# Weight loads by a list of units, and query rows loaded two pairs ahead

## The chip, the core and the metric

The kernel runs on one core of a Trainium2 chip. The core has five engines that run at the same time and wait for one another through semaphores: PE (TensorE, matrix products; its weight loads are shown as PEld), DVE (VectorE), ACT (ScalarE), POOL (GpSimd) and SP (SyncE, which here only issues transfers). Transfers between the large memory (DRAM) and the on-chip memory (SBUF) run on 16 DMA engines. SP, ACT and POOL each issue transfers in the order of their own instructions: an instruction that waits holds up all that stand behind it on its engine.

The metric is the device time of one execution in microseconds (us); lower is better.

## What is computed

Two independent parts, joined along the last axis. Part A is a long convolution (an SSM layer): a shift filter on k, a product with v, a convolution over the sequence of 2048 with ssm_k, and a product with q. Part B is a recurrent attention over 64 segments of 32 rows, each of which carries 8 memory rows on to the next.

```python
def _A_ref(q, k, v, shift_k, ssm_k, ssm_D):
    ...
    kv = k_shift * v
    ...
    kv_f = rfft(kv_pad); kf_f = rfft(kf_pad)
    y = irfft(kv_f * kf_f)[:, :S, :]
    y = y + kv * ssm_D[None, None, :]
    return q * y

def _B_ref(x, mem0, Wq, Wk, Wv, Wo, seg_len):
    ...
    for s in range(n_seg):
        h = concat([mem, x[:, s * 32:(s + 1) * 32]])
        q, k, v = h @ Wq, h @ Wk, h @ Wv
        p = softmax(mask(q @ k.T * scale))
        o = (p @ v) @ Wo
        mem = o[:, :M]; outs.append(o[:, M:])
```

## The kernel before

Part A is a Fourier transform in factors, in three stages, each a loop over tiles of 128 rows. Stage 1 (`a_kernel`, up to about 105 us) transforms the rows of u = kv and of the filter and stores them to DRAM as SU1 and SK1. Stage 2 (lines 290 to 399) has 17 sets; for each set SP gathers four tiles of 0.26 MB (Kg and Ug, three buffers each), and the set is worked on in two halves. One half is called a unit here, so there are 34, numbered 0 to 33. A unit has a front (PE makes Kre, Kim, Ure and Uim in PSUM, ACT and DVE multiply them, POOL makes Yre, DVE makes Yim) and a back, one unit later (PE makes z_ps from Yre and Yim, ACT copies it to zs; after the second half ACT stores zs to SZ in DRAM). Stage 3 (lines 401 to 422) has 16 tiles: SP loads zt from SZ (0.52 MB; all of SZ must be there, as each zt reads a strip across all sets), PE makes y_ps with four matmuls, DVE multiplies it with the query rows qt, and POOL stores the product of two tiles at a time (ot to out). A qt holds the query rows of two tiles, a pair.

Between these PE does work of part B. `fill` (line 675) is called once per unit in stage 2 and once per tile in stage 3, and counts its calls in n: n = 0 to 33 are the units, n = 34 to 49 the tiles. Each call stores one finished piece of the dense part (RKQ, on ACT), may copy a weight from SBUF to a scratch in DRAM (WS, on POOL), may load a weight (`load_next`, line 659), transposes x rows at every third n (`x_block`, xt_ps on PE, stored to REC by POOL; X_sb is loaded by `x_load` two blocks at a time), and advances the generator `rest` by one to three slices. A slice is four matmuls kb_ps on PE. `rest` runs four dense groups: Wk first half, Wk second half, Wq first half, Wq second half, 32 slices each, and each needs eight weights of 0.52 MB.

The first group's weights are loaded by POOL at the end of stage 1. The other 24 are in `plan` (line 649), in the order in which the groups need them, with a home for each: tiles Wmid, which stay; three spare tiles; ring tiles pw; and last the tile wring2, which holds x rows (X_sb) as long as stage 2 lasts. `stage1_done` issues four of the 24 loads and twelve slices ahead of unit 0. `fill` issues the others by a rule (line 686): at each n below 34 that doesn't leave 2 on division by 3, as long as more than two are left, and the last two at n = 37 and 38. The load is placed behind the newest gather on SP. Loads of weights that are streamed later are followed by their copy to WS at an odd n; a copy waits for its load.

PE's order in stage 2 is written out by hand (`manual_schedule`). All other orders are made by a scheduler from the program and the tiles' lifetimes: PE's in stage 3, and SP's, POOL's, DVE's and ACT's everywhere. A tile that takes over the place of an older one waits until that one's readers and writers are done; stage 3's pools take the places of stage 2's, and the homes of the Wv weights (Wres, Wmore, loaded by SP after the last zt) those of stage 3's.

After stage 3 PE finishes the dense groups and computes vb_ps from the Wv weights (line 775). From about 383 us on the recurrence of part B runs, 64 segments, in which PE streams weights that stay in SBUF and 13 per segment that SP loads anew (wring from WS).

Of the kernel before, what the change touches and what calls it, by code (L numbers as in the profile page):

```python
# [9 lines left out]
BF = mybir.dt.bfloat16  # L10
# [18 lines left out]
STREAM = (0, 8, 15, 19, 24, 31, 36, 41, 45, 51, 52, 54, 56, 57, 58, 63)  # L29
N2, N3 = 12, 19  # L30
WO_COPY = 29
AHEAD, REST_LOAD = 12, (37, 38)
X_LOAD = 1
STAGE3 = 34
LATE_RING = 5
# [17 lines left out]
def a_kernel(ctx: ExitStack, tc, q, k, v, shift_k, ssm_k, ssm_D, outa, ps_sum, slot4, slot16, stage1_done, fill):  # L53
    nc = tc.nc
# [18 lines left out]
    def pair_rows(ap2d, t):  # L73
        return ap2d.rearrange("(p r) d -> p (r d)", r=16)[:, 1024 * t:1024 * t + 2048]

    with ExitStack() as c1:
        cw = c1.enter_context(tc.tile_pool(name="a_cw", bufs=1, side="right"))
        io = c1.enter_context(tc.tile_pool(name="a1_io", bufs=2, side="right"))
# [320 lines left out]
            unit_back(*pending)  # L399

    with ExitStack() as c3:
        io = c3.enter_context(tc.tile_pool(name="a3_io", bufs=4, side="right"))
        wk = c3.enter_context(tc.tile_pool(name="a3_wk", bufs=4, side="right"))
        ps_big = c3.enter_context(tc.tile_pool(name="a3_ps", bufs=3, space=PSUM))
        xp = c3.enter_context(tc.tile_pool(name="a3_x", bufs=2, side="right"))
        for t in range(16):
            pt = ps_big.tile([128, 1024], F32, tag="big", name="y_ps")
            zt = io.tile([128, 2, 1024], BF, tag="zt", bufs=5, name="zt")
            nc.sync.dma_start(zt[:], SZ.rearrange("m (r h) d -> r m h d", h=2)[t])
            for hf in range(2):  # L410
                for h in range(2):
                    nc.tensor.matmul(pt[:, hf * 512:(hf + 1) * 512], lhsT=G2h[h][:, :],
                                     rhs=zt[:, h, hf * 512:(hf + 1) * 512], start=(h == 0), stop=(h == 1))
            if t % 2 == 0:
                qt = io.tile([128, 2048], BF, tag="qt", bufs=3, name="qt")
                nc.sync.dma_start(qt[:], pair_rows(q, t))
                ot = wk.tile([128, 2048], BF, tag="ot", name="ot")
            half = slice(1024 * (t % 2), 1024 * (t % 2) + 1024)
            nc.vector.tensor_tensor(out=ot[:, half], in0=pt[:], in1=qt[:, half], op=ALU.mult)
            if t % 2:  # L420
                nc.gpsimd.dma_start(outa.rearrange("(p r) d -> p r d", r=16)[:, t - 1:t + 1, :],
                                    ot[:].rearrange("p (r d) -> p r d", r=2))
            fill(pool=xp)


def b_kernel(ctx: ExitStack, tc, x, mem0, Wq, Wk, Wv, Wo, outb, n_seg, run_a):
    nc = tc.nc
# [28 lines left out]
    def dram_chunk(ch):  # L456
        m, a, g = ch
        return Wo_v[a] if m == 3 else W_v[m][a, g]

    def dst_view(ap, ch):  # L460
        return ap.rearrange("p (hh d) -> p hh d", hh=2) if ch[0] == 3 else ap

    def stream_src(ch):
        return WS[ring_order.index(ch), :, 0:2048]
# [47 lines left out]
    def stage1_done(su, vl, spare):  # L512
        make_consts()
        pools["mid"] = ctx.enter_context(tc.tile_pool(name="b_wmid", bufs=1, reuse_waits="tile"))
        for i, ch in enumerate(parts[0]):
            res[ch] = pools["mid"].tile([128, 2048], BF, name=f"Wmid{i}")[:]
        make_xbt(su)
        ws = [None] * 8
        for kc in range(8):
            with tc.issue_after(vl[1 + kc // 3].ins):  # L520
                group(0, 0, which=[kc], ws=ws, eng=nc.gpsimd)
        weights[0, 0] = ws
        plan_loads(spare)
        for _ in range(4):
            load_next()
        for _ in range(AHEAD):
            next(rest)

# [31 lines left out]
    def make_xbt(su):  # L560
        xb = x.rearrange("(tb s t) d -> tb s t d", s=16, t=SEG)
        for tb in range(4):
            X_sb = pair()[:, 0:1024]
            with tc.issue_after(su[X_LOAD + tb].ins):
                nc.sync.dma_start(X_sb, xb[tb, :, NX:SEG, :])
            tp = ps0.tile([128, 1024], BF, tag="ps0", name="xbt_ps")
            for kc in range(8):
                nc.tensor.transpose(tp[:, kc * 128:(kc + 1) * 128], X_sb[:, kc * 128:(kc + 1) * 128], ident[:])
            for h in range(2):
                nc.scalar.copy(XBT[h][:, :, 16 * tb:16 * tb + 16, :].rearrange("p k s t -> p k (s t)"),  # L570
                               tp[:, 512 * h:512 * h + 512].rearrange("p (k c) -> p k c", k=4))
# [3 lines left out]
    def group(m, g, temps={}, which=range(8), ws=None, eng=nc.sync, held=False):  # L575
        ws = ws or [None] * 8
        for kc in which:
            ch = (m, kc, g)
            if ch in res:
                got.append(eng.dma_start(res[ch], dram_chunk(ch)))  # L580
                ws[kc] = res[ch]
            else:
                t = temps[ch]() if ch in temps else pw()
                got.append(eng.dma_start(t[:], dram_chunk(ch)))
                if ch in streamed:
                    copies.append((stream_src(ch), t[:]))
                ws[kc] = t[:]
        while copies and not held:
            copied.append(nc.gpsimd.dma_start(*copies.pop(0)))
        return ws  # L590
# [4 lines left out]
    def x_load(b, pool=None):  # L595
        t = pool.tile([128, 2048], BF, tag="X_sb", name="X_sb") if pool else base.tile([128, 2048], BF, tag="wring2", name="X_sb")
        x_loads.append(nc.sync.dma_start(t[:].rearrange("p (b d) -> p b d", b=2),
                                         x[b * 128:(b + 2) * 128, :].rearrange("(b p) d -> p b d", b=2)))
        loaded[b], loaded[b + 1] = t[:, 0:1024], t[:, 1024:2048]
# [42 lines left out]
    plan = []  # L642

    def plan_loads(spare):
        pws = iter((4, 5, 6, 7, 0, 1))
        temps = iter([lambda: spare(0), lambda: spare(1), lambda: spare(2), lambda: pw(3), lambda: pw(2),
                      lambda: base.tile([128, 2048], BF, tag="wring2", name="pw")])
        for m, g in ((0, 1), (1, 0), (1, 1)):
            for kc in sorted(range(8), key=lambda kc: (m, kc, g) not in placed):
                ch = (m, kc, g)  # L650
                plan.append((ch, (lambda k=next(pws): pw(k)) if ch in kept_q1 else None if ch in placed else next(temps)))

    def load_next(ins=None):
        ch, home = plan.pop(0)
        m, kc, g = ch
        if ch in kept_q1:
            res[ch] = home()[:]
        with tc.issue_after(ins) if ins is not None else ExitStack():
            group(m, g, {ch: home}, [kc], weights[m, g], held=True)
# [8 lines left out]
    def store():  # L668
        if stores:
            nc.scalar.dma_start(*stores.pop(0))  # L670
# [5 lines left out]
    def fill(behind=None, pool=None):  # L676
        store()
        n = units[0]
        units[0] += 1
        if n == 0:  # L680
            x_load(0)
        if n >= WO_COPY and wo_copies:
            ch = wo_copies.pop(0)
            with tc.issue_after(rec_stores[-1].ins):
                nc.gpsimd.dma_start(dst_view(stream_src(ch), ch), dram_chunk(ch))
        if n in REST_LOAD or n < STAGE3 and n % 3 != 2 and len(plan) > len(REST_LOAD):
            load_next((behind or x_loads[-1]).ins)
        if n > 5 and n % 2 and copies:
            with tc.issue_after(rec_stores[-1].ins):
                copied.append(nc.gpsimd.dma_start(*copies.pop(0)))  # L690
        if n % 3 == 2 and blocks:
            b = blocks.pop(0)
            x_block(b, pool)
            if b % 2 and blocks:
                x_load(b + 1, pool)
        for _ in range(3 if n >= STAGE3 else 1 if n % 3 == 2 else 2):
            next(rest, None)

    run_a(ps0, pw, slot16, stage1_done, fill)

    wres3 = ctx.enter_context(tc.tile_pool(name="b_wres", bufs=1, reuse_waits="tile"))
# [463 lines left out]
def kernel(  # L1165
# [23 lines left out]
    def run_a(ps_sum, slot4, slot16, stage1_done, fill):  # L1189
        with ExitStack() as ctx_a:  # L1190
            a_kernel(ctx_a, tc, A_q[0], A_k[0], A_v[0], A_shift_k, A_ssm_k, A_ssm_D, outa, ps_sum, slot4, slot16, stage1_done, fill)
# [41 lines left out]
```

## Time and profile before

| | us |
|---|---|
| three runs | 1717.8, 1718.3, 1725.6 |
| their median | 1718.33 |
| the profiled run | 1718.1 |
| its span, first to last instruction | 1716.2 |
| PE busy in the span | 1639.0 (96%) |
| DVE busy | 1031.3 (60%) |
| ACT busy | 681.3 (40%) |
| POOL busy | 349.9 (20%) |
| mean DMA rate | 348 GB/s |

Times in a profile count from the first instruction. A busy time is the sum over an engine's instructions; matmuls overlap, so a busy PE can have short gaps inside. "Idle before" is the time for which an engine stood still just ahead of an instruction, and behind the arrow stands what released it. The chain of waits follows the end of the program back to the beginning, at each step to whatever came last. A table of windows gives for each stretch of time its length, the busy time of each engine with the number of instructions, the granted clock of PE as a share of full speed, the mean share of time in which the 16 DMA engines were busy (somewhat over 1.00 is possible, as packets overlap), and the bytes that they moved. For a DMA the profile gives the time from its issue to its landing.

### The profile page before, as it was taken

The numbers are of one execution on the slowest core, as the hardware profiler recorded it, in microseconds if no ns is written. First come the engines' busy times: TensorE is split into PE (matmuls) and PEld (weight loads), VectorE is DVE, ScalarE is ACT, GpSimd is POOL, SyncE is SP. The second block draws the span as 40 slices with busy tenths as digits, with TensorE's granted clock in tenths as the row PEclk, the third lists the DMA queues.
The fourth block names the chain that finished last, engine by engine and source line by source line (L and its number), as shares of the span: only waits on it lengthen the run. The fifth ranks groups of instructions, "written<-read, shape, count | busy, mean of one in ns | idle before, by whom it ended". The sixth has DMA issues, their size and how long they took to land.

```text
span 1716.2 us, 71129 instructions
## 1 busy us (share of the span) xinstructions
PE 1639.0 (96%) x30744; PEld 998.9 (58%) x30776; DVE 1031.3 (60%) x3454; ACT 681.3 (40%) x1259; POOL 349.9 (20%) x626
## 2 busy tenths in 40 slices
PE   6888898999999999999999999999999999999998
PEld 3433333445666666666666666666666666666665
DVE  9947873235555665665565555565665556555555
ACT  6876661103333333433333333333333333333333
POOL 4103341101212121121121121211211211212111
PEclk9999999999999999999999999999999999999999
DMA  9989989989999999999999999999999999999997
GB/s 332 378 321 366 384 291 411 381 319 381 351 338 355 355 351 344 358 349 350 353 344 346 339 344 351 352 355 337 357 355 340 346 340 361 350 346 352 340 330 282
DMA packets 180830, 598.03 MB, mean 348 GB/s; under 512 B 24658, under 2 KB 24674, under 8 KB 180516
## 3 DMA queue, kind: packets, MB, share of 16 engines
q1 hardware_dynamic: 151860, 525.80, 84.4%
q0 software_dynamic: 19984, 44.61, 7.4%
q10 hardware_dynamic: 8672, 23.07, 3.4%
q8 instruction: 241, 3.95, 0.9%
q14 instruction: 73, 0.60, 0.1%
HBM read 538.33 MB, written 57.15 MB: 347 GB/s over the span
## 4 chain that ended last, share of the span: by engine, by line
PE 80%; DMA 10%; DVE 3%; ACT 3%; issue 3%; POOL 1%; SPq 0%; ACTq 0%; another core or an unknown queue 0%; DVEq 0%; POOLq 0%
PE acc L967 36%; PE yacc L1061 27%; PE kb_ps L630 4%; PE vb_ps L775 2%; DMA zt<-SZ 2%; DMA wring<-WS 2%; PE OTp L989 2%; DMA out_dram<-arena 2%; PE OTp L1039 2%; PE OTp L905 1%; ACT s_sb L249 1%; DMA Ug<-SU 1%; PE s_ps L247 1%; PE SB L995 1%; PE ks_ps L285 1%
## 5 line engine op out<-in xcount | busy, mean ns | idle before, releaser
L967 PEld LDWEIGHTS <-rec 128*32 128x32 bf16 x12288 | 301.7, 96 | 278.2 <-DVE rec L916 37.6
L1061 PEld LDWEIGHTS <-arena 128*64 128x64 bf16 x8255 | 430.2, 109 | 54.1 <-ACT arena L1051 32.7
L980 ACT CAST arena<-acc 128x512 bf16<-128x512 f32 x320 | 187.1, 585 | 357.3 <-PE acc L967 347.7
L967 PE MATMUL acc<-Wres,rec 128*32 128x512 bf16 x3328 | 252.7, 380 | 0.7 <-issue 0.7
L967 PE MATMUL acc<-wring,rec 128*32 128x512 bf16 x2300 | 229.5, 380 | 4.6 <-DMA wring<-WS 1.8
L967 PE MATMUL acc<-Wmid,rec 128*32 128x512 bf16 x3072 | 211.8, 379 | 0.2 <-issue 0.2
L1061 PE MATMUL yacc<-Wmore,arena 128*64 128x256 bf16 (+1 forms) x2560 | 209.5, 273 | 0.2 <-issue 0.2
L1051 ACT CAST arena<-OTp 128x640 bf16<-128x640 f32 x128 | 88.6, 692 | 204.7 <-PE OTp L1043 185.1
L1092 DVE COPY arena<-OTp 128x512 bf16<-128x512 bf16 x64 | 27.2, 425 | 229.3 <-PE OTp L905 229.3
L1061 PE MATMUL yacc<-wring,arena 128*64 128x256 bf16 x2064 | 160.0, 274 | 3.1 <-DMA wring<-WS 2.5
L813 DVE TENSOR_SCALAR arena<-OTp 128x256 int32<-128x256 int32 x378 | 128.1, 394 | 37.1 <-ACT arena L1051 34.7
L1061 PE MATMUL yacc<-arena 128*64 128x256 bf16 x1071 | 140.1, 270 | 0.1
L1158 ACT CAST arena<-yacc 128x256 bf16<-128x256 f32 x128 | 47.7, 373 | 228.7 <-PE yacc L1061 225.4
L967 PE MATMUL acc<-pw,rec 128*32 128x512 bf16 x1796 | 122.3, 379 | 1.6 <-issue 1.5
L946 POOL DMA_DIRECT2D arena<-VBD x128 | 68.6, 536 | 261.2 <-DVE arena L1006 94.8
L967 PE MATMUL acc<-Wlate,rec 128*32 128x512 bf16 x1536 | 117.0, 381 | 0.0
L916 DVE CAST rec<-tps 128x32 bf16<-128x32 f32 x128 | 24.5, 192 | 149.7 <-PE tps L914 148.6
L1160 POOL DMA_DIRECT2D out_dram<-arena x128 | 66.0, 516 | 203.9 <-ACT arena L1158 200.2
L900 POOL DMA_DIRECT2D arena<-RKQ x64 | 49.7, 777 | 257.1 <-PE yacc L1061 248.1
L1004 DVE TENSOR_REDUCE mx<-SB 128x8 f32<-128x320 f32 x128 | 62.6, 489 | 49.3 <-PE SB L998 46.3
L895 POOL DMA_DIRECT2D rec<-REC x64 | 36.0, 563 | 244.4 <-PE acc L967 240.4
L1009 ACT ACTIVATE arena<-arena 128x320 f32<-128x320 f32 x128 | 60.3, 471 | 64.2 <-DVE arena L1006 60.2
(222 smaller groups left out, 2628.5 us busy)
## 6 DMA issues: line engine op xcount, KB each, us to landing
wring<-WS SPq DMA_DIRECT2D x831, 512.0 KB, 5.9
SK<-s_sb SPq DMA_DIRECT2D x16, 512.0 KB, 7.4
SU<-s_sb SPq DMA_DIRECT2D x16, 512.0 KB, 6.4
Kg<-SK SPq DMA_DIRECT2D x32, 256.0 KB, 6.2
Ug<-SU SPq DMA_DIRECT2D x32, 256.0 KB, 6.5
RKQ<-stage ACTq DMA_DIRECT2D x16, 512.0 KB, 8.2
zt<-SZ SPq DMA_DIRECT2D x16, 512.0 KB, 10.2
arena<-RKQ POOLq DMA_DIRECT2D x64, 128.0 KB, 5.7
```

Source lines behind the costliest of these rows:

```text
L630: nc.tensor.matmul(ps[:], lhsT=ws[kc][:, hl * 128:(hl + 1) * 128], rhs=xbt(kc).rearrange("p s t -> p (s t)"), start=(kc == 0), stop=(kc == 7))
L813: nc.vector.tensor_scalar(out=dst, in0=src, scalar1=0, scalar2=None, op0=ALU.bitwise_or)
L900: nc.gpsimd.dma_start(rec.rearrange("p (j c) -> p j c", j=4), RKQ[s // 16, :, :, s % 16, :].rearrange("j p c -> p j c"))
L946: nc.gpsimd.dma_start(VB, VBD[g, s].rearrange("t h e -> h t e"))
L967: nc.tensor.matmul(self.acc[32 * c:32 * c + 32, :], lhsT=hT[:, ch[1], :], rhs=w[:, 512 * c:512 * c + 512], start=(ch == chs[0]), stop=(ch ...
L980: nc.scalar.copy(sb, self.acc[:])
L1004: nc.vector.tensor_reduce(out=mx[:], in_=S, op=ALU.max, axis=AX.X)
L1009: nc.scalar.activation(E, E, ACT.Exp, scale=scale)
L1051: nc.scalar.copy(OT, o_view)
L1061: nc.tensor.matmul(yacc[f][64 * dh:64 * dh + m, x - o:y - o], lhsT=lhsT, rhs=r, start=(h == (0, 2 * FIRST[-1])[f] and x == o), stop=stop, ...
L1158: nc.scalar.copy(Y[:, 256 * f:256 * f + 256], yacc[f][:, 0:256])
L1160: nc.gpsimd.dma_start(bass.AP(outb.tensor, outb.offset + SEG * s * 2048 + 512 * dh, [[2048, 32], [1, 512]]), Y[64 * dh + NM:64 * dh + 40, :])
```

## The change

The rule for the weight loads is replaced by a list, `LOAD_AT`, with one entry per load: the n at which it is issued. The four loads in `stage1_done` are gone; units 28 to 33 each have an entry, unit 33 two, and the last load is at n = 35. In stage 3 the pools are entered in another order: ot's pool first, then a new pool for qt with three buffers that waits by the tile, then zt's with five buffers, and x rows last as before. Two qt are loaded ahead of the loop and, at each even tile t up to 10, the one for the pair t + 4; before, each pair's qt was loaded behind its first zt.

```diff
-AHEAD, REST_LOAD = 12, (37, 38)
+AHEAD = 12
+LOAD_AT = (0, 1, 2, 3, 4, 6, 8, 10, 12, 14, 16, 18, 20, 22, 24, 26, 28, 29, 30, 31, 32, 33, 33, 35)
...
     with ExitStack() as c3:
-        io = c3.enter_context(tc.tile_pool(name="a3_io", bufs=4, side="right"))
         wk = c3.enter_context(tc.tile_pool(name="a3_wk", bufs=4, side="right"))
+        qp = c3.enter_context(tc.tile_pool(name="a3_q", bufs=3, side="right", reuse_waits="tile"))
+        io = c3.enter_context(tc.tile_pool(name="a3_io", bufs=5, side="right"))
         ps_big = c3.enter_context(tc.tile_pool(name="a3_ps", bufs=3, space=PSUM))
         xp = c3.enter_context(tc.tile_pool(name="a3_x", bufs=2, side="right"))
+        def q_load(t):
+            qt = qp.tile([128, 2048], BF, tag="qt", name="qt")
+            nc.sync.dma_start(qt[:], pair_rows(q, t))
+            return qt
+
+        qts = [q_load(0), q_load(2)]
         for t in range(16):
             pt = ps_big.tile([128, 1024], F32, tag="big", name="y_ps")
-            zt = io.tile([128, 2, 1024], BF, tag="zt", bufs=5, name="zt")
+            zt = io.tile([128, 2, 1024], BF, tag="zt", name="zt")
...
             if t % 2 == 0:
-                qt = io.tile([128, 2048], BF, tag="qt", bufs=3, name="qt")
-                nc.sync.dma_start(qt[:], pair_rows(q, t))
+                qt = qts.pop(0)
+                if t < 12:
+                    qts.append(q_load(t + 4))
                 ot = wk.tile([128, 2048], BF, tag="ot", name="ot")
...
         plan_loads(spare)
-        for _ in range(4):
-            load_next()
         for _ in range(AHEAD):
             next(rest)
...
-        if n in REST_LOAD or n < STAGE3 and n % 3 != 2 and len(plan) > len(REST_LOAD):
+        for _ in range(LOAD_AT.count(n)):
             load_next((behind or x_loads[-1]).ins)
```

## The prediction

> **What bounds the kernel now.** I read the chain of waits first, then busy time by stage, then the PE's waits in the stages touched, then the DMA share in 4 us steps. The chain (start, length, what) runs through loads in two places only:
>
> ```profile
> 145.88 6.12 DMA Ug<-SU
> 154.25 7.20 DMA Ug<-SU
> 161.52 6.39 DMA Ug<-SU
> ...
> 191.58 8.53 DMA X_sb<-in_B_x_dram
> 255.12 12.24 DMA zt<-SZ
> 267.42 17.28 DMA zt<-SZ
> 284.77 9.99 DMA zt<-SZ
> ```
>
> The first four lie in stage 2, up to about unit 20; the last three in stage 3. From 200 to 248 us, and again after 295 us, the chain lies almost wholly on compute. The stages as windows (length, then busy us of PE, PEld, DVE, ACT, POOL; granted clock; DMA share; GB/s):
>
> ```profile
> 120.00:247.70 127.70, 115.64 (x707) 44.37 (x719) 105.51 (x192) 85.04 (x162) 53.04 (x55) 0.99 0.97 353
> 247.70:323.75 76.05, 68.18 (x329) 31.19 (x336) 23.72 (x28) 17.48 (x30) 10.94 (x18) 0.98 0.98 382
> ```
>
> In stage 2 (120.0 us, first Kre_ps, to 247.7 us, end of the last z_ps) PE idles 127.70 - 115.64 = 12.1 us; from there to the first vb_ps, 7.9 us. DMA is as full as PE. What PE waits for (line, us, times, longest), and the worst single wait on PE and POOL:
>
> ```profile
> PE z_ps L377 <- POOL Yre L367: 6.4, 7, 2.9
> PE y_ps L412 <- DMA zt<-SZ: 7.3, 5, 3.4
> ```
>
> ```profile
> 181.16 0.54 POOL L690 DMA_DIRECT2D WS<-pw  x1 [3.57 <-DMA pw<-in_B_Wq_dram]
> 181.72 1.16 POOL L367 TENSOR_TENSOR Yre<-pa,pb 128x512 bf16<-128x512 bf16 x1
> ```
>
> ```profile
> 182.93 0.39 PE L377 MATMUL z_ps<-Yre,Nre 64*128 64x512 bf16 x2 [2.90 <-POOL Yre L367]
> ...
> 183.47 3.00 PE L630 MATMUL kb_ps<-XBT,Wmid 128*128 128x512 bf16 x7
> ```
>
> POOL's copy of a streamed weight waits for that weight's load (issued 174.32), and Yre of unit 15 stands behind it. PE loses 2.90 us, and then runs at a granted clock of 0.61: seven kb_ps take 3.00 us where the next such group takes 1.69. DMA by 4 us steps (share, then GB/s, at the end):
>
> ```profile
> 216.00:220.00 4.00, 4.00 (x28) 1.42 (x25) 3.40 (x6) 3.24 (x8) 1.15 (x1) 1.00 1.05 403
> 220.00:224.00 4.00, 3.66 (x26) 1.49 (x25) 4.00 (x9) 2.77 (x6) 2.96 (x3) 1.00 0.74 268
> 224.00:228.00 4.00, 4.00 (x24) 1.57 (x23) 3.93 (x8) 2.98 (x6) 3.85 (x6) 1.00 0.37 90
> 228.00:232.00 4.00, 3.63 (x29) 1.56 (x30) 3.96 (x7) 2.88 (x6) 2.36 (x3) 1.00 0.62 242
> 232.00:236.00 4.00, 3.92 (x26) 1.49 (x24) 3.97 (x9) 3.03 (x7) 2.56 (x4) 1.00 0.79 235
> ...
> 248.00:252.00 4.00, 3.77 (x25) 1.92 (x23) 0.76 (x2) 1.48 (x4) 0.57 (x1) 1.00 0.65 215
> ```
>
> There is a hole between the last gathers (222 us) and the first zt (250 us), because SP holds nothing but one X_sb until SZ is complete. Free share over 220 to 252 us: 4 x (0.26+0.63+0.38+0.21+0.04+0.35) = 7.5 us. Everywhere else from 108 to 316 us the share is 0.92 or more.
>
> **The change, part by part.** The sum goes against the profiled run's own 1718.1 us (span 1716.2 and 1.9 around it); the median shown is 1718.33.
>
> *Loads in stage 2.* No load is added or dropped: 24 of 0.524 MB, each 1.30 us of all DMA engines at 403 GB/s. Before, four go at set-up and 18 more by unit 25; after, none at set-up, 10 by unit 15 (15 before), 15 by unit 25 (22 before), seven at units 28 to 33, one at 35. In the built order SP issues two of the seven ahead of the last gathers and five behind, into the hole. So up to unit 15 five loads, 6.5 us of DMA, no longer lie ahead of the gathers. What PE can win there: idle 12.1, plus the slow clock (3.00+0.63 us for eight kb_ps instead of 1.69+0.38) 1.6, is 13.7 us. From 200 to 248 us, where nothing of DMA is in the chain, about 1.4 us of waits remain over 14 units, so 3.4 us over 34 are the engines' own. Removable: 10.2 us. One part is sure by position: the pw copy now stands behind Yre27, three units after its load, where it had stood one unit after it; that is 2.9 + 1.6 = 4.5 us. The other 5.7 us hang on gathers and X_sb being late, and 6.5 us of earlier traffic is gone. I take 3.5 of them, since five loads now fall on units 18 to 26 at full PE pace. Term: -8.0 (bounds 0 and -10.2).
>
> *Are the moved weights in time?* The last weight of the second dense group is loaded at unit 10 and first read in unit 12. In the trace the load of unit 10 was issued at 152.0 us and unit 12's slice began at 165.6 us: 13.6 us of cover, against at most 8.5 us for a spare load to land. Those of units 28 to 35 are read from the 103rd kb_ps after the last z_ps on, 285.6 us in the trace. On POOL the copy of one of them stands ahead of Yre33 (244.8 us), some 17 us after its load's place in the hole, and that of the last ahead of the first out store. Cost nothing; with a cover gone, a late weight costs PE its lateness once.
>
> *The hole.* Seven loads are 9.1 us of DMA in 7.5 free; 1.6 us spill toward stage 3. They are issued within a few us of 222 and the next thing that PE waits for, X_sb at 231 us for unit 32 (240.3 us), has 9.3 us. Counted with stage 3.
>
> *Stage 3, bytes.* PE is held last by zt of tile 11 (it lands at 294.8 us); behind it both orders are PE-bound, with 112 kb_ps to the first vb_ps in each. Counted on SP from the first load of stage 3, tile 11 is the 22nd half megabyte in both orders. What leaves the stretch are other queues' bytes: the copy of one pw load to WS (0.52 MB), and part of the four RKQ stores (2.1 MB, issued at 285 to 288 us), which follow the 103rd kb_ps, now one tile later in PE's order; I take half, 1.05 MB. 1.57 MB at 0.41 MB/us is -3.8 us, and the spill +1.6. Term: -2.2 (bounds +1.6 and -7.3, the whole zt wait).
>
> *Query rows ahead.* They do not reach the hole: SP has the load of unit 35 ahead of them, which shares its buffer with the x rows and waits for the transposes of x block 11, at 249.2 us in the trace. So three loads (pw, qt, qt) now stand ahead of the first zt: 3.9 us later. Cover: 40 kb_ps before the first y_ps where there were 27, 13 x 0.216 = 2.8 us, and five zt buffers. From the third pair on, qt(t+4) waits for the multiply of tile t-1, and zt(t+2) is queued behind it. By the rows, a tile takes 3.05 us of PE (262.14, 265.16, 268.19), its multiply begins 1.06 us after its matmuls and takes 1.22: zt(t+2) is issued 2.8 us after y(t-1) and due at 9.1, so it has 6.3 us. Three loads (3.9 us) and an out store (1.3), over a fixed part of about 1.3 (a 64 KB scatter landed in 1.6), make 6.5. Five such pairs, 0.2 each: +1.0 (bounds 0 and 19.5, see the rivals). The wait for qt on DVE (15.2 us, five times) goes; it held no PE.
>
> *Stage 4's first weights.* With the pools turned round, the fifth Wv load waits for the last out store, where before later ones did; PE waited 0.3 us for these. Out stores land in 7.6 us, so the load comes at most some 2.5 us later than its 317.8 us, for a use at 325.5 us; behind it on SP stand three more Wres that the first vb_ps groups read. Term +0.1 (0 to 2.5).
>
> Sum: -8.0 - 2.2 + 1.0 + 0.1 = -9.1; 1718.1 - 9.1 = **1709.0 us**. The recurrence from 383 us has the same order on every engine and moves as a block.
>
> **Rivals.** *Both waits go* (1702.9): the stage 2 term, and all 7.3 us of zt waits: -8.0 - 7.3 + 0.1. For it: qt leaves DVE's path and 13 more kb_ps stand in front. Against: DMA stays at 1.02 to 1.04 in that stretch.
>
> *The wait comes back elsewhere* (1713.5): the spare copy to WS now stands ahead of Yre9, and its load follows the gathers that unit 7 releases, the same two units as pw's load had before Yre15. If it lands as late, 4.5 us return. Against: the four set-up loads (5.2 us) are gone by then.
>
> *The last scatters land late* (1716.4): if the moved loads still fill the engines at 248 us, the last SZ store, 1.6 us when DMA was quiet, takes the 9.0 of the one issued at 136.83; +7.4. Against: by the sum the spill is 1.6 us. [...]
>
> *Slower: qt stops zt* (1727.5). If a zt lands in the median 10.2 us of now, and not in 6.5, each of the five pairs costs 10.2 - 6.3 = 3.9 us, 19.5 in all, instead of +1.0: -9.1 + 18.5 = +9.4. It decides from a landing over 6.3 us. For it: no zt landed in under 8.3 us. Against: they landed so late behind five to seven queued loads; after, at most three stand there.
>
> **How the numbers follow.** Forecast 0.43 (own range 1704 to 1713), both waits 0.16, wait comes back 0.18, scatters 0.06, slower 0.17. About 0.5% (8.6 us) is what a measurement of this kernel can tell. Faster beyond it (under 1709.7): 0.26 of the forecast and 0.16, 0.42. Within: 0.17 + 0.18 + 0.06 = 0.41. Slower: 0.17. The range, 1701 to 1726, leaves out the slower case and little below.
>
> **What would show it.** Stage 2 from first Kre_ps to last z_ps near 120 us instead of 127.7, no z_ps wait near 2.9 us; DMA share over 0.9 in the 15 us after the last gathers; first y_ps some 9 us after the last z_ps (7.0 before); qt waits gone from DVE; zt landing in 6 to 7 us. It is wrong if stage 2 keeps its length, if zt waits on PE exceed 7.3 us, or if SP stands at qt with the DMA share under 0.8.

## The result, and the profile after

| | before | after |
|---|---|---|
| median of 22 runs each, us | 1719.68 | 1728.68 |
| lowest to highest, us | 1713.68 to 1732.66 | 1717.29 to 1740.85 |
| ratio, 95% interval | | 1.0049, 1.0034 to 1.0064 |

The changed kernel is slower by half a per cent, 8 to 9 us, where 9.1 us less was forecast. The profiled run of after happens to be its quickest (1717.3 us) and that of before is an ordinary one (1718.1 us), so their totals say nothing; the stages do. The recurrence has the same order of instructions in both and takes 1324 to 1342 us in the profiled runs of this study, in no relation to the edits; 1333.3 us is that of before, 1323.9 of after. What is ahead of it went from 262.9 to 269.7 us (first Kre_ps to the first product of the recurrence).

The windows of after, by the same stages as before, and one more up to the recurrence (length, then busy us of PE, PEld, DVE, ACT, POOL; granted clock; DMA share; GB/s):

```profile
121.80:251.10 129.30, 116.14 (x719) 44.40 (x719) 106.10 (x192) 84.89 (x162) 53.59 (x56) 0.97 0.98 360
251.10:329.55 78.45, 68.59 (x335) 30.79 (x335) 23.44 (x28) 17.49 (x30) 10.31 (x16) 0.98 0.94 350
329.55:391.50 61.95, 57.77 (x266) 25.41 (x264) 22.69 (x35) 0.59 (x1) 4.31 (x8) 0.97 0.90 335
```

Stage 2 takes 129.3 us instead of 127.7, from there to the first vb_ps 78.5 instead of 76.1, and from there to the recurrence 62.0 instead of 59.2 (323.75 to 382.90 in before). In the second of these the DMA share fell from 0.98 to 0.94: the engines that move the data stood still more often, in a stretch in which before's chain of waits ran through loads of zt. What PE waits for in after, from stage 2 to the first vb_ps:

```profile
PE y_ps L420 <- DMA zt<-SZ: 5.3, 5, 1.4
PE xt_ps L615 <- DMA X_sb<-in_B_x_dram: 4.6, 2, 4.3
PE y_ps L420 <- DMA qt<-in_A_q_dram: 3.8, 1, 3.8
...
PE z_ps L378 <- POOL Yre L368: 2.9, 4, 1.0
```

The wait of 2.90 us for Yre is gone (the longest is 1.0), and zt holds PE for 5.3 us instead of 7.3. In their place stand two others: 4.3 us for x rows (0.8 in before), and 3.8 us ahead of the first y_ps, which before did not have. DMA in steps of 4 us, and PE's own rows at the first of the two waits:

```profile
228.00:232.00 4.00, 2.99 (x19) 1.16 (x18) 4.00 (x9) 3.11 (x7) 1.71 (x2) 1.00 1.03 411
...
240.00:244.00 4.00, 1.66 (x10) 1.13 (x11) 0.77 (x3) 0.00 (x0) 0.27 (x1) 0.52 0.97 391
244.00:248.00 4.00, 4.00 (x12) 1.12 (x11) 1.86 (x5) 1.52 (x3) 1.13 (x2) 0.63 0.51 198
...
252.00:256.00 4.00, 3.77 (x24) 1.93 (x23) 0.76 (x2) 1.45 (x3) 0.58 (x1) 1.00 0.69 181
```

```profile
242.34 1.03 PE L615 MATMUL xt_ps<-ident,X_sb 128*128 128x128 bf16 x8 [4.30 <-DMA X_sb<-in_B_x_dram]
243.17 1.91 PE L637 MATMUL kb_ps<-XBT,Wmid 128*128 128x512 bf16 x4
```

The hole of before from 220 us on is filled (1.00 to 1.04 in every step up to 240 us, 0.97 in the next). The X_sb load is issued at 227.67 us behind five weight loads that SP issued from 219.64 to 224.72, and lands after 14.6 us, where before it took 4.0. Up to unit 28 the gain is there: its Yre stands 6.0 us earlier, counted from the first Yre, than in before; at unit 32 4.1 us of it are left. Then PE stands 4.30 us, and the two steps from 240 us show a granted clock of 0.52 and 0.63; over the 4 us right behind the wait (242.34 to 246.34) it is 0.50, by my estimate another 2.0 us of PE (half of the 4). Two shorter waits were followed by a low clock too: 2.90 us in before (0.59 over the 4 us behind it) and 2.58 us in loads_only, a run below (0.66; its 12 us from 232 to 244 us show 0.86, those on either side 1.00). 244 to 256 us is now the hole (0.51 to 0.71). What SP did next, as its timeline in after:

```profile
253.05 0.33 SPq L591 DMA_DIRECT2D pw<-in_B_Wq_dram  x1
253.48 1.21 SPq L410 DMA_DIRECT2D qt<-in_A_q_dram  x2
254.98 0.50 SPq L417 DMA_DIRECT2D zt<-SZ  x1
255.53 0.74 SPq L410 DMA_DIRECT2D qt<-in_A_q_dram  x1
...
259.17 0.81 SPq L417 DMA_DIRECT2D zt<-SZ  x2
270.45 0.33 SPq L410 DMA_DIRECT2D qt<-in_A_q_dram  x1
270.83 0.90 SPq L417 DMA_DIRECT2D zt<-SZ  x2
```

The first zt is issued at 254.98 us, 4 us behind the last z_ps (250.06, under 3 us behind, in before), since the last Wq load waited for x block 11 and two qt stand ahead of the zt. And after the fourth zt SP issues nothing for over 10 us (259.98 to 270.45): it stands at a qt load that waits for DVE's multiply, with the fifth zt behind it. There are five such waits, 29.0 us together; before had none.

### The profile page after: what moved, and what is told of

The parts are those of the page before. It is cut to its first block, busy times and chain, and to the rows that moved or that the text cites. A ratio compares the mean times of both kernels' runs of the same rounds, so it can differ in the third digit from the quotient of the medians.

```text
span 1715.4 us, 71164 instructions
## 1 busy us (share of the span) xinstructions
PE 1640.1 (96%) x30776; PEld 991.0 (58%) x30776; DVE 1031.7 (60%) x3454; ACT 681.9 (40%) x1259; POOL 349.9 (20%) x626
## 4 chain that ended last, share of the span: by engine, by line
PE 84%; DMA 8%; DVE 3%; ACT 2%; issue 2%; SPq 0%; POOL 0%; ACTq 0%; POOLq 0%; DVEq 0%
PE acc L974 38%; PE yacc L1068 27%; PE kb_ps L637 4%; PE vb_ps L782 3%; PE OTp L996 2%; DMA X_sb<-in_B_x_dram 2%; DMA wring<-WS 2%; PE OTp L1046 2%; PE OTp L912 2%; PE s_ps L248 1%; PE ks_ps L286 1%; DMA out_dram<-arena 1%; ACT s_sb L250 1%; DMA zt<-SZ 1%; DMA Kg<-SK 1%
## 5 line engine op out<-in xcount | busy, mean ns | idle before, releaser
L974 PEld LDWEIGHTS <-rec 128*32 128x32 bf16 x12288 | 293.4, 96 | 283.5 <-DVE rec L923 38.0
## 6 DMA issues: line engine op xcount, KB each, us to landing
zt<-SZ SPq DMA_DIRECT2D x16, 512.0 KB, 10.5
```

Source lines behind the costliest of these rows:

```text
L974: nc.tensor.matmul(self.acc[32 * c:32 * c + 32, :], lhsT=hT[:, ch[1], :], rhs=w[:, 512 * c:512 * c + 512], start=(ch == chs[0]), stop=(ch ...
```

## The experiments

The expectations spell their theories out; in the text these go by letters. Q: the lead of two pairs in stage 3 is the loss, as SP stands at the qt loads with zt loads behind them. X: the gain of stage 2 is lost at X_sb, behind the crowded weight loads. S: stage 3 starts late, behind the last Wq load. P and W: what follows stage 3 is late, by the pools' layout (P) or by a weight copy on POOL that holds output stores and REC stores (W). B: the bytes set it all, whatever the order. R: the recurrence itself. Each ratio is to before, timed beside it on the same chip.

**The same kernel again.**

> The changed kernel as it is, for a second profile on the chip of the runs below. Theory X (an x rows' load, X_sb, stands on SP behind five weight loads in the hole, so PE waits for it in unit 32) and theory Q (in stage 3 the loads of weight and qt stand ahead of zt) both expect the loss before the recurrence: first acc about 8 us later than in the kernel before (391 against 383 us), with a PE wait of 4 us for X_sb, a wait of about 4 us before the first y_ps, and SP held at qt for some 29 us in sum. Rival R (the recurrence itself is slower) expects the first acc at 383 to 386 us and the 9 us behind it.

Measured: ratio 1.0065, 1.0041 to 1.0089. Kre_ps to the recurrence 275.2 us, SP at qt 30.5 us, X_sb 5.5 us in two waits (3.5 at x block 10). So the loss is there again, ahead of the recurrence; and two profiles of one kernel differ by 5.5 us in that stretch, so that one profile does not settle a difference of 2 or 3 us.

**Each half of the change alone.** loads_only has the list and stage 3 of before; stage3_only has the rule of before and stage 3 of after.

> The list of loads alone, stage 3 as before. X: PE still waits 4 us or more for X_sb in unit 32 and the last z_ps is as late as in the changed kernel (251 us); the time lies 3 to 6 us above before. Q: the loss is gone, the time lies 3 to 8 us under before, as stage 2's earlier waits are shorter. R: the same as before within 2 us.

> Stage 3's pools and qt ahead alone, loads by the old rule. X: no wait for X_sb, the last z_ps at 247 to 248 us, the time the same as before within 3 us. Q: SP is held at qt for 20 to 30 us in sum, zt waits on PE above 7.3 us, the time 4 to 8 us above before. R: the same as before within 2 us.

Measured: loads_only 0.9992 (0.9972 to 1.0012), stage3_only 1.0048 (1.0028 to 1.0069). The product, 1.0040, is about the whole. So the list nets nothing and stage 3's edit carries the loss. In loads_only stage 2 takes 126.2 us (127.3 in before, both from the first Kre_ps to the start of the last z_ps), with 2.9 us of waiting for X_sb; z_ps to vb_ps is 4 us shorter, and vb_ps to the recurrence 4 us longer. Its time is neither X's nor Q's, but within 2 us of before. In stage3_only z_ps to vb_ps is 5.4 us longer than in before, SP stands 25.6 us at qt and zt holds PE for 8.3 us, as Q had it; R falls with this run.

**X_sb ahead of the crowded loads.**

```diff
-            load_next((behind or x_loads[-1]).ins)
+            load_next((x_loads[-1] if n >= 30 else behind or x_loads[-1]).ins)
```

> The changed kernel with the loads from unit 30 on placed behind the x rows' load of unit 29, so that X_sb goes ahead of five weight loads. X: the wait for X_sb and the slow clock behind it go, 5 to 7 us less than the changed kernel, 2 to 4 us above before. Q: at most 2 us less than the changed kernel, as the start of stage 3 stays as it is. R: no difference to the changed kernel.

Measured: 1.0058 (1.0037 to 1.0078). The wait for X_sb at x block 10 is gone (4.30 us in after; 1.6 us at an earlier block remain), and the load is issued at 227.5 us (227.67 in after), with the first Kre_ps at 121.8 us in both; so its place on SP is what had made it late there. But a weight that now lands later has its copy on POOL ahead of unit 33's Yre, and that wait grew to 6.1 us. The wait moved; X could be neither kept nor dropped by this run.

**Less lead for the query rows, or one buffer more**, in three ways: one pair ahead (q_one); two ahead with a fourth qt buffer taken from zt (q_four); and one ahead with the last Wq load at n = 38 (q_one_38).

```diff
 # q_one
-        qts = [q_load(0), q_load(2)]
+        qts = [q_load(0)]
...
-                if t < 12:
-                    qts.append(q_load(t + 4))
+                if t < 14:
+                    qts.append(q_load(t + 2))
```

```diff
 # q_four
-        qp = c3.enter_context(tc.tile_pool(name="a3_q", bufs=3, side="right", reuse_waits="tile"))
-        io = c3.enter_context(tc.tile_pool(name="a3_io", bufs=5, side="right"))
+        qp = c3.enter_context(tc.tile_pool(name="a3_q", bufs=4, side="right", reuse_waits="tile"))
+        io = c3.enter_context(tc.tile_pool(name="a3_io", bufs=4, side="right"))
```

> After, with the query rows loaded one pair ahead instead of two: SP reaches a qt load two pairs later, when the multiply that frees its buffer is long done. Theory Q (SP stands 26 to 30 us at five qt loads, with zt loads queued behind them): SP waits at L410 for DVE under 5 us, z to vb falls from 79 us to 73 to 75 us, the time to 1723 to 1726. Theory S (the loss is the late start of stage 3, the last Wq load waiting for x block 11 ahead of the first zt): z to vb stays 78 to 80 us, 1729 to 1731. Theory P (the new layout of the pools holds the loads of Wv): z to vb falls, and what it falls comes back between vb and the recurrence; 1728 to 1731.

> After, with four query buffers and four zt buffers in place of three and five, so the same bytes and the same order of loads, but a qt load waits for a multiply of two pairs earlier. Theory Q: the wait of SP for DVE at L410 goes from 30 us to under 3 us, z to vb falls by 3 to 5 us, 1724 to 1727; if four zt buffers are too few, SP waits for y_ps at the zt loads instead, over 10 us, and the time stays at 1729. Theory S: no change, 1729 to 1731.

> q_one, and the last load of Wq at n = 38 instead of 35, so that SP issues the first qt and zt without waiting for x block 11's landing and transposes. Theory Q and S together: the first y_ps comes 8 to 11 us behind the last z_ps (13.8 in after), and the time falls 2 to 4 us below q_one, to 1719 to 1723. Theory Q alone: same as q_one within 1.5 us, the start being made up at the end of stage 3, where DMA bytes set the time.

Measured: q_one 1.0009 (0.9988 to 1.0030), q_four 1.0026 (1.0002 to 1.0049), q_one_38 1.0003 (0.9978 to 1.0027). The times came where Q put them; that of q_four is not clear of after's, as the intervals overlap. The traces did not: SP still stands 21.6 us at qt in q_one (under 5 were expected), 14.3 in q_four (under 3) and 18.9 in q_one_38, and z_ps to vb_ps is 78.2 us in q_one, where S had put it and not Q (73 to 75). SP runs ahead of PE by as many tiles as there are zt buffers, so it meets a qt load early and waits there in any case. The sum of SP's waits is therefore not the price. What differs is what a wait is for. By the buffer that it takes over, the qt load issued at tile t waits in after for the multiply of tile t - 1, in q_one and q_four for that of tile t - 3; so it holds the zt loads behind it for two tiles less. q_one_38 has the first y_ps 9.3 us behind the last z_ps, as S said (13.8 in after, 12.4 in q_one), and wins nothing that the interval shows.

**The layout alone.** Everything of after, but each qt load back behind the zt of its pair.

```diff
-        qts = [q_load(0), q_load(2)]
...
-                qt = qts.pop(0)
-                if t < 12:
-                    qts.append(q_load(t + 4))
+                qt = q_load(t)
```

> After with each query load back in the place that before has it (behind the zt of its pair), so that only the list of weight loads and the new layout of stage 3's pools are left. Theory Q (the lead of two pairs, and SP standing at the qt loads for it, is the loss): SP does not wait for DVE at qt at all, z to vb is 72 to 75 us as in loads_only, the time 1718 to 1721, ratio 0.998 to 1.001. Theory P (the layout of the pools delays the output stores and the loads of Wv): vb to the recurrence 62 to 65 us and a ratio of 1.003 to 1.006.

Measured: 1.0004 (0.9984 to 1.0023). SP does not wait for DVE at qt at all, zt holds PE for 0.8 us, and z_ps to vb_ps is 73.3 us. So the layout by itself does not make the loss; the lead does. (vb_ps to the recurrence is long, 66.0 us, as P had it, but the time is not.) The windows of after and then of pools_only in the stretch where SP stands:

```profile
264.00:272.00 8.00, 7.12 (x32) 3.05 (x33) 3.11 (x4) 0.59 (x1) 1.02 (x2) 0.79 0.92 332
272.00:280.00 8.00, 6.28 (x30) 2.57 (x28) 3.68 (x3) 1.17 (x2) 1.01 (x2) 1.00 0.96 348
280.00:288.00 8.00, 6.88 (x38) 3.06 (x37) 4.33 (x5) 1.62 (x3) 1.32 (x2) 1.00 0.93 368
```

```profile
264.00:272.00 8.00, 6.28 (x34) 2.99 (x35) 3.20 (x4) 1.17 (x2) 1.31 (x2) 1.00 1.03 419
272.00:280.00 8.00, 7.57 (x40) 3.38 (x38) 3.68 (x3) 1.76 (x3) 1.44 (x2) 1.00 1.03 413
280.00:288.00 8.00, 7.86 (x39) 3.47 (x38) 3.11 (x4) 1.76 (x3) 1.29 (x2) 1.00 1.03 414
```

349 GB/s on the mean against 415: over these 24 us after moves 1.6 MB less, three loads. The same over the whole of stage 3, from first to last y_ps, in after, q_four, pools_only and before:

```profile
264.60:317.30 52.70, 46.89 (x230) 20.87 (x231) 21.02 (x23) 9.86 (x17) 8.03 (x13) 0.97 0.99 383
263.50:314.00 50.50, 46.57 (x226) 21.01 (x231) 21.02 (x23) 9.83 (x17) 8.41 (x13) 0.97 1.03 409
258.30:309.30 51.00, 48.40 (x244) 21.98 (x245) 21.11 (x23) 11.00 (x19) 6.24 (x10) 1.00 1.02 412
254.70:311.40 56.70, 49.37 (x238) 22.60 (x244) 21.30 (x23) 10.95 (x19) 8.60 (x14) 0.97 1.03 411
```

By the last figure of such rows all profiles fall into two groups: 376 to 385 GB/s in the five with a lead of two pairs and three buffers, 398 (q_one) to 413 in the nine others. This fits Q: what the lead costs in the middle of stage 3 is loads that are not under way.

**The list made better**, with stage 3 of before: the last load at n = 38 (loads_38); X_sb first as well, and no copy at n = 31 and 33 (best_x); the loads of n = 30 to 35 spread out, two of them at n = 33 and four at 35 to 38 (best_spread). In SP's order the two of n = 33 come ahead of X_sb, unlike what the expectation says, so that two loads stand directly ahead of it there, where five do in after.

```diff
 # best_spread
-LOAD_AT = (..., 24, 26, 28, 29, 30, 31, 32, 33, 33, 35)
+LOAD_AT = (..., 24, 26, 28, 29, 33, 33, 35, 36, 37, 38)
```

> loads_only (stage 3 of before) with the last load of Wq at n = 38. Theory S: the first zt no longer stands behind that load, first y_ps 7 to 9 us behind the last z_ps (10.1 in loads_only), 1715 to 1718, faster than both kernels. Theory B (stage 3 and Wv are set by the bytes that must move between the last z and the recurrence): as loads_only, 1719 to 1721.

> loads_38 with x blocks 10 and 11 loaded ahead of the last five Wq loads of stage 2, and with no copy of weight chunks on POOL at n = 31 and 33, so that it cannot stand ahead of unit 33's Yre as it did in x_first. Theory X (the gain of stage 2 is lost at the 4 to 5 us wait for x block 10 and the slow clock behind it): that wait falls under 2 us, no POOL wait over 2 us behind unit 28, stage 2 takes 123 to 126 us, and the time falls to 1712 to 1715, ratio 0.995 to 0.997. Theory B (the bytes between the gathers' end and the recurrence set it): first Kre to the recurrence stays 262 to 264 us, 1716 to 1719.

> Stage 3 of before, with only two of the six crowded Wq loads left ahead of x block 10 (n = 28 and 29), two at 33 and the other four at 35 to 38. Theory X: the wait for x block 10 falls under 2 us and stage 2 takes 124 to 126 us; the 2 MB of weights that go into stage 3 cost there 0 to 3 us; 1714 to 1718, ratio 0.996 to 0.999. Theory B: 1719 to 1722, since the bytes that leave the hole before the last z have to move behind it.

Measured: loads_38 0.9980 (0.9959 to 1.0000), best_x 1.0002 (0.9983 to 1.0021), best_spread 0.9979 (0.9964 to 0.9995), with 1718.0 us against 1723.4. In loads_38 the first y_ps is 7.4 us behind the last z_ps, as S said, while x block 10 still costs 4.6 us. best_x missed X's mark: no wait for X_sb above 2 us, but one of 5.8 us for Yre in its place. best_spread has neither:

```profile
120.00:242.80 122.80, 114.30 (x718) 43.42 (x718) 104.61 (x192) 85.28 (x162) 52.96 (x55) 1.00 0.99 362
242.80:320.70 77.90, 67.91 (x337) 30.92 (x337) 23.63 (x28) 17.48 (x30) 11.32 (x18) 1.00 1.01 394
320.70:378.80 58.10, 56.01 (x270) 25.15 (x272) 22.60 (x35) 0.59 (x1) 3.73 (x7) 1.00 0.92 340
```

```profile
235.46 0.62 PE L607 MATMUL xt_ps<-ident,X_sb 128*128 128x128 bf16 x8
```

These are its windows by stage and its row of x block 10 on PE: no wait ahead of it, at full clock. Stage 2 takes 122.8 us, 4.9 less than in before; the stretch to vb_ps takes 1.9 us more, with the four loads in it, at a share of 1.01. It is the one version whose interval lies below 1, by a small margin. That the 4.9 us of stage 2 are what it wins is not shown: loads_38, with 129.9 us to the start of its last z_ps (122.5 in best_spread), has the same ratio.

**The copy on POOL.** In after the first copy of a Wv weight to WS waits for its load, and the last output stores and REC stores stand behind it:

```profile
315.10 0.58 POOL L596 DMA_DIRECT2D WS<-pw  x1 [11.05 <-DMA pw<-in_B_Wv_dram]
315.78 0.71 POOL L430 DMA_DIRECT2D out_dram<-ot  x1
316.48 0.58 POOL L620 DMA_DIRECT2D REC<-xt  x1
```

SP holds a Wres load for that REC store (11.1 us), with Wmore behind it. But before has the same order and nearly the same waits, 11.5 us of SP among them:

```profile
309.78 0.58 POOL L589 DMA_DIRECT2D WS<-pw  x1 [9.83 <-DMA pw<-in_B_Wv_dram]
```

```diff
-            copied.append(nc.gpsimd.dma_start(*copies.pop(0)))
+            with tc.issue_after(rec_stores[-1].ins) if m == 2 else ExitStack():
+                copied.append(nc.gpsimd.dma_start(*copies.pop(0)))
```

> After, with the copies of Wv chunks to the stream scratch issued behind the last REC store on POOL, so that the first of them no longer holds the last output stores and REC stores for 11 us while it waits for a weight load. Theory W (the Wv loads that SP holds until the last REC store are late because of that copy): POOL does not wait for pw of Wv ahead of the last REC store, SP's wait for REC falls from 11 us to 3 to 7 us, DMA share over 0.9 in the 15 us behind the last y_ps, PE waits under 1.5 us in all for Wres and Wmore in vb_ps (2.6 to 3.9 in after and its repeat), vb to the recurrence 58 to 60 us, ratio 1.002 to 1.004. Theory B (that stretch is set by the bytes, whenever they are asked for) or theory Q alone: vb to the recurrence 61 to 65 us, ratio 1.004 to 1.007.

Measured: 1.0023 (1.0003 to 1.0044). The output and REC stores are issued at 310.40 and 311.12 us, PE's waits for Wres in vb_ps come to 1.6 us, vb_ps to the recurrence takes 61.0 us, and SP still waits 8.8 us for REC. The time is W's; of the marks in the trace some lie between the theories and the wait for REC misses W's. The interval overlaps those of after. So some of the loss may lie there; how much stays open. Alone this copy can't make a kernel slower than before: it waits 13.0 us in loads_only and in pools_only, with the last output and REC stores behind it, and neither is slower.

All profiles together, in us, grouped by what stage 3 does with the query rows (each figure from one profiled run, from the first Kre_ps, the start of the last z_ps, the first vb_ps and the first product of the recurrence):

| | z_ps to vb_ps | Kre_ps to the recurrence | ratio |
|---|---|---|---|
| two pairs ahead, three buffers: after, after_again, stage3_only, x_first, after_copy | 78.8, 79.6, 81.9, 81.5, 79.4 | 269.7, 275.2, 268.9, 271.8, 269.0 | 1.0049, 1.0065, 1.0048, 1.0058, 1.0023 |
| same layout, less lead or a fourth buffer: q_one, q_four, q_one_38, pools_only | 78.2, 76.6, 75.1, 73.3 | 265.2, 265.1, 263.2, 265.9 | 1.0009, 1.0026, 1.0003, 1.0004 |
| stage 3 of before: before, loads_only, loads_38, best_x, best_spread | 76.5, 72.5, 74.0, 75.5, 78.2 | 262.9, 261.8, 263.6, 262.2, 258.8 | 1, 0.9992, 0.9980, 1.0002, 0.9979 |

The first group lies above the two others in both stretches, in the first by 0.6 us only; among the ratios after_copy lies below q_four. By the means of the second column the lead of two pairs with three buffers costs some 6 us (270.9 against 264.9). Counted from the last z_ps to the recurrence, where stage 3's order can act, it is 142.1 against 137.8, or 4.4 us (135.1 in the third group); the rest is stage 2, where the groups' orders are the same and the waits scatter.

## Why the prediction was wrong

*Loads in stage 2, -8.0.* The mechanism held up to unit 28: 6.0 us earlier, no long wait at Yre. Stage 2 as a whole still took 1.6 us more than in before. The step that failed is the one under "The hole", that X_sb "has 9.3 us" and so costs nothing. It was weighed by the bytes of the hole as a whole; what counted was the queue ahead of one load. Five loads, at the 1.30 us that I had for each, are 6.5 us; added to the quiet landing of 4.0 they make 10.5, over the cover of 9.3 unless some have landed by then. Measured were 14.6 us, 4.3 us of waiting and 4 us at a clock of 0.50. The 1.30 us also supposed all DMA engines for SP: of the 11.0 MB moved from 215 to 243 us SP's queue had 5.4, the stores and copies of ACT and POOL the rest. In the nine profiles with this list and these five loads ahead of X_sb, Yre of unit 28 starts 3.3 to 7.6 us earlier than in before, that of unit 33 from 1.5 us earlier to 3.1 us later. best_spread, with two loads in the place of the five, got 4.9 us in stage 2. The sure part of 4.5 us was right up to unit 28; of the other 3.5 some 1.5 came. Not all of the rest is X_sb: in q_one it landed after 9.5 us, with no wait, and Yre of unit 33 was still only 1.5 us earlier.

*The spill of 1.6 us and stage 3's bytes, -2.2.* With the list and without the lead (loads_only, pools_only) z_ps to vb_ps fell by 4.0 and 3.2 us, and in loads_only the stretch moved 27.3 MB instead of 29.2 (its length times its rate), so the bytes left it about as forecast. But vb_ps to the recurrence grew by 4.0 and 6.9 us, and in both the time did not fall. The sum counted what these bytes give in one stretch and not what the next takes back; why it takes it back isn't shown.

*Query rows ahead, +1.0.* This is the step that made the forecast's sign wrong in stage 3. zt landed in a median 10.5 us and not in the 6.5 of my sum, close to the 10.2 of before: I had taken few queued loads to mean a quick landing. The waits for zt in the middle of stage 3 nevertheless came to 5.3 us, less than before's 7.3. What I had set at nothing is the start: the three loads ahead of the first zt, said to be covered by 13 more kb_ps. PE waited 3.8 us there, and the first y_ps came 13.8 us behind the last z_ps instead of the 9 forecast (7.4 in before; the forecast counted from the end of z_ps, 0.4 us later). That wait is put down to qt, but the two qt were issued just ahead of the first zt on the same queue, and no instruction of y_ps reads them. In all z_ps to vb_ps is 2.3 us longer in after, with a list that alone makes it 4.0 shorter. How the loss divides between start and middle isn't settled: q_one_38 took away the late start and q_one nearly nothing of it, and their times are the same.

*Wv weights, +0.1.* vb_ps to the recurrence is 2.8 us longer in the profile of after and 5.2 in its repeat, over the upper bound of 2.5. I counted the wait for the last output store and not what stood ahead of that store on POOL, a copy that waits 11 us for a weight. But the copy stands there in before as well (9.8 us), and loads_only, with the old pools, has the stretch 4.0 us longer too; so neither the copy nor the new layout is shown to be the cause. By the intervals, the loss that after_copy takes away lies anywhere from nothing to nearly all.

Of the rivals, the wait did not come back at unit 9, and the last scatters held nothing (the last SZ store landed after 1.6 us in after, as in before). The slower case, qt stopping zt, came within 1.2 us of the measured median (1727.5) and named the right part; its working was off. Its 19.5 us in the five pairs were not there (5.3 us of zt waits in all), and the 8.0 us that it left standing in stage 2 were not there either. Two errors cancelled. Of the signs that I had listed, three came: no long z_ps wait, the filled hole, DVE free of qt. The three that did not come, stage 2 at 120 us, the first y_ps at 9 us, zt landing in 6 to 7 us, are those that carried the forecast. Of the signs of being wrong the first came: stage 2 kept its length. The time in the recurrence moved as a block, as said, but its own scatter is as large as all that was sought here.

## What to carry to other kernels

The hole in the DMA share was not free here: X_sb, which PE needed, stood behind five other loads, landed after 14.6 us instead of 4.0, and PE waited 4.30 us. So count the queue ahead of the next load that PE waits for, on its own issuing engine, and add its quiet landing time, before filling the hole. A load issued further ahead needs the buffers for its lead; with too few, the qt loads of after waited for multiplies that were only just coming up (five waits, 29.0 us), the zt loads behind them on SP went out late, and 349 GB/s moved where 415 did without the lead. How long the issuing engine stands is not the price by itself (14 to 22 us of it were in kernels at 1.0003 to 1.0026): look at whether the data engines run short. Move loads a few at a time around such a point: the list with four of its loads moved behind the needed x rows won 4.9 us in the stage where the crowded one lost 1.6, though its ratio is no better than that of the list with only the last load moved.

## What the runs showed of the hardware that was not expected

A 0.52 MB load behind five others landed after 9.5 to 15.2 us in nine profiles (median 13.9; 14.6 in after, 9.5 in q_one), against 4.0 us in the quiet stretch of before. By the median that is some 2 us for each load ahead, more than the 1.30 us of its bytes at 403 GB/s; the other queues moved data at the same time (5.6 of the 11.0 MB from 215 to 243 us in after). Two of the waits at this spot cost PE more than their length: 4.30 us of standing in after were followed by a clock of 0.50 over the next 4 us, and 2.58 us in loads_only by one of 0.66. Not every wait did: 3.23 us ahead of the first y_ps in loads_only were followed by 1.00 (256 to 264 us).
